# Attention and a gated feed-forward in one kernel: rests of two pairs as one group scaled on VectorE, two chunks of scores ahead of the rests at the first norm, and the output weights' sums on GpSimd

## The chip, the cores and the metric

The kernel runs on one core of a Trainium2 chip, in float32. The metric is the device time of one execution in microseconds; lower is better. The core has five engines with queues of their own: TensorE (matrix products; PE in the profile, PEld for its weight loads), VectorE (DVE), ScalarE (ACT), GpSimd (POOL) and SyncE (SP, which here issues nearly all transfers). Each runs its own instructions in the order in which the program gave them and waits for the others by semaphores. TensorE writes to PSUM, the others work on SBUF and, but for GpSimd, on PSUM.

## The reference

Queries and keys are normalised over the head, attention follows, and its output, put back into rows, goes through a normalised SwiGLU feed-forward.

```python
batch, n_heads, seq, head_dim = (8, 12, 448, 64)
n_tokens, d_model, d_ff = (3584, 768, 1536)

q_n, k_n = (rmsnorm(q, g_q), rmsnorm(k, g_k))
scores = scale * np.matmul(q_n, k_n.transpose(0, 1, 3, 2))
scores = scores - np.max(scores, axis=-1, keepdims=True)
attn = np.exp(scores)
attn = attn / (np.sum(attn, axis=-1, keepdims=True) + 1e-09)
out = np.matmul(attn, v)
...
xn = x / rms * rms_g
g = xn @ w_gate
silu = g * (1.0 / (1.0 + np.exp(-g)))
val = xn @ w_val
return silu * val @ w_out
```

## The kernel before

The work is cut into 48 pairs of heads, six to each of the 8 sequences (`g` counts pairs, `b, hp = divmod(g, 6)`). A pair's 448 positions are three full blocks of 128 and a rest of 64. The rests of all six pairs of a sequence lie in one tile, `rest`, and so they are normalised together, in groups.

The order of the work is written out by hand. A list of steps on TensorE is made with `pe(fn)`; `after(n, fn)` puts the work of another engine n steps later in the program. An engine's queue is therefore in the order of these calls, whatever the data are doing.

For each pair, `squares` (L461) squares q and k on ScalarE (L470), sums on VectorE (L473) and calls `rms_qk` on GpSimd (L489, L490: the reciprocal root) and `norm_q` (L492), which scales the three blocks of q with two GpSimd products (L495). k is not scaled; its factor goes into the exponential. `norm_rests(b, lo, hi)` (L439) does the same for the rests of pairs lo to hi of a sequence: squares L446, sums L448, the root L451 and L452, and the scaling of q and k L453, the last three on GpSimd. `turn(g, i)` (L499) transposes q with its rests (i = 0: L511, L513; the copies are qT, L514 on ScalarE, and the rests' part of kT, L515 on VectorE) or the blocks of k (i = 1, copy L517).

`score(g, chunks)` (L519) multiplies k and q for chunks of 128 keys, two matmuls each (one for each head, L527), into PSUM tiles of `ps_s`, of which there are four, and ScalarE takes the exponential (L531). `rests(g)` (L552) does this for the 64 last keys of pair g (L557, exponential L572, one tile of `ps_s`) and begins the output of pair g-1 (L563; in the first seven pairs also the sums of exponentials, L568). That output is collected in the one tile of `ps_m`. `values(g)` (L574, L579) adds the other keys, `sums(g)` (L582, L592) the sums of exponentials over the keys. VectorE takes their reciprocal (L596 or L600) and scales the output into `x` (L607), which frees the tile of `ps_m`; ScalarE squares x (L610, L612) and GpSimd adds that up (L613). From pair 7 on the exponentials are added on GpSimd before the sums (L537, L544).

When a sequence's six pairs are done, `rms_x` (L622) and `norm_x` (L633) normalise x: four matmuls (L627), the root (L629, L631), four matmuls that spread it over the partitions (L639), and six products on VectorE (L646). This happens for the first time at pair 7. Then the feed-forward's matmuls come, in pieces that `fill` places between the steps of the attention.

During the first sequences the feed-forward's weights, which are given in float64, are converted in pieces of 128x384 (`convert`, L753: ScalarE L719 and L720, VectorE L725 to L727, GpSimd L763) and stored in DRAM (`kept`, `kept_o`). The first sequence's feed-forward multiplies plainly (L1107, L973). All the later ones use Strassen's scheme with seven products (`quad`, L883, products L878; `out_strassen`, L1012, products L1076). It needs weights that are sums of blocks: those of the gate and value weights are made by `derive` (L822, subtraction L835), those of the output weights by `derive_o` (L843, subtraction L855). They are made once, while the second sequence's feed-forward runs, and stored; derive_o makes four for each of six columns, 24 in all, each 128x384, and each store (L751) waits in SyncE's queue for its subtraction. In the same stretch VectorE adds products (L890), does the gate (L900, L901) and adds blocks of the feed-forward's hidden values (L953 to L956, 128x128), for the output's scheme.

The start, before the loop over the pairs, is:

```python
    squares(0, 0)
    warm(9)
    pe(idle)
    norm_rests(0, 0, 1)
    squares(0, 1)
    pe(lambda: turn(0, 1))
    gains()
    squares(1, 0)
    squares(1, 1)
    warm(3)
    pe(lambda: turn(0, 0))
    norm_rests(0, 1, 3)
```

`warm` issues matmuls on the identity (L1223).

Of the kernel before, what the change touches and what calls it, by code (L numbers as in the profile page):

```python
# [12 lines left out]
ALU = mybir.AluOpType  # L13
# [5 lines left out]
B, H, S, D = 8, 12, 448, 64  # L19
# [3 lines left out]
NPAIR = H // 2  # L23
# [312 lines left out]
def safe_scores(  # L336
# [20 lines left out]
    nc = tc.nc  # L357
# [21 lines left out]
    def after(n, fn):  # L379
        due.append((now["t"] + n, fn))  # L380

    def pe(fn):
        now["t"] += 1
        fn()
        for item in [d for d in due if d[0] <= now["t"]]:
            due.remove(item)
            item[1]()


    NG = B * NPAIR  # L390
# [4 lines left out]
    def own(j):  # L395
        return slice(j * D, (j + 1) * D)
# [42 lines left out]
    def norm_rests(b, lo, hi):  # L439

        if b >= B:
            return
        n = hi - lo
        rest = st["rest", b][:, lo:hi]
        sq = tmp.tile([128, n, 2, D], F32, name="sq", tag="sq", bufs=2)
        nc.scalar.activation(sq, rest, ACT.Square)  # L446
        ms = small.tile([128, n, 2], F32, name="msr")
        after(1, lambda: nc.vector.tensor_reduce(out=ms, in_=sq, axis=AX_X, op=ALU.add))  # L448

        def scale():  # L450
            nc.gpsimd.tensor_scalar(ms, ms, D * 1e-6, None, ALU.add)  # L451
            nc.gpsimd.tensor_tensor(ms, ms, mhalf[:, 0:2 * n].rearrange("p (n h) -> p n h", h=2), ALU.pow)  # L452
            nc.gpsimd.tensor_tensor(rest, rest, ms.unsqueeze(3).to_broadcast([128, n, 2, D]), ALU.mult)  # L453

        after(1 if b == 0 else 2, scale)

    def direct(g):
# [3 lines left out]
    def squares(g, i):  # L461

        if g >= NG:
            return
        n = 2 * NK
        if i == 0:
            st["ms", g] = small.tile([128, 2 * n], F32, name="ms")
        ms = st["ms", g]
        sq = tmp.tile([128, n * D], F32, name="sq", tag="sq", bufs=2)
        nc.scalar.activation(sq, st["qk", g][:, i], ACT.Square)  # L470

        def reduce():
            nc.vector.tensor_reduce(out=ms[:, i * n:(i + 1) * n], in_=sq.rearrange("p (n d) -> p n d", d=D), axis=AX_X, op=ALU.add)  # L473

        after(1, reduce)
        if g <= 1:

            after(1, lambda: rms_qk(g, slice(i * n, (i + 1) * n)))
            if i == 0:
                after(1, lambda: norm_q(g))  # L480
        elif i == 1:
            after(2, lambda: rms_qk(g))
            after(2, lambda: norm_q(g))
# [8 lines left out]
    def norm_q(g):  # L492
        qn = st["qn", g] = qn_pool.tile([128, 2 * NK * D], F32, name="qn")
        for h in range(2):
            nc.gpsimd.tensor_tensor(  # L495
                qn.rearrange("p (t h d) -> p h t d", h=2, d=D)[:, 1 - h], st["qk", g][:, 0].rearrange("p (h t d) -> p h t d", h=2, d=D)[:, h],
                st["rs", g][:, h * NK:(h + 1) * NK].unsqueeze(2).to_broadcast([128, NK, D]), ALU.mult)

    def turn(g, i):  # L499


        if g >= NG:
            return
        b, hp = divmod(g, NPAIR)
        if ("qT", g) not in st:
            for part in ("qT", "kT"):
                st[part, g] = qkT_pool.tile([128, S], F32, name=part)
        src = st.pop(("qn", g)) if i == 0 else st["qk", g][:, 1]
        ps = (ps_m if todo else ps_f).tile([128, 512], F32, name="tr", tag="m" if todo else "f")
        for t in range(NK):  # L510
            nc.tensor.transpose(ps[:, t * 128:(t + 1) * 128], src[:, t * 2 * D:(t + 1) * 2 * D], ident)  # L511
        if i == 0:
            nc.tensor.transpose(ps[:, NK * 128:], st["rest", b][:, hp].rearrange("p h d -> p (h d)"), ident)  # L513
            nc.scalar.activation(st["qT", g], ps[:, 0:S], ACT.Copy, scale=gqk[:, 0:1])  # L514
            nc.vector.tensor_copy(st["kT", g][:, LAST], ps[:, S:])  # L515
        else:
            nc.vector.tensor_copy(st["kT", g][:, FULL], ps[:, FULL])  # L517
# [56 lines left out]
    def values(g):  # L574

        vt, av = st["v", g], st["av", g]
        for c in range(NK):
            for j in range(2):
                nc.tensor.matmul(av[own(j), 0:S], lhsT=vt[:, j, c], rhs=st["e", g, c, j], start=False,  # L579
                                 stop=(c == NK - 1), skip_group_check=True)  # L580
# [123 lines left out]
    def data(key):  # L704
        return st[key][0][:, 0:BW]
# [137 lines left out]
    def derive_o(wait=6):  # L843

        if not sums_o:
            return
        c, (to, plus, minus, place) = sums_o[0]
        for name in BLOCKS:
            if asked.get(("wd", 1, name, c), now["t"]) > now["t"] - wait:
                return  # L850
        sums_o.pop(0)
        a, b = data(("wd", 1, plus, c)), data(("wd", 1, minus, c))
        key = ("wd", 1, to, c)
        st[key] = st[("wd", 1, place, c)]
        nc.vector.tensor_tensor(data(key), a, b, ALU.subtract)  # L855

        def store():
            keep(key)
            asked["sums_o"] = asked.get("sums_o", 0) + 1

        after(1, store)
        if to == "T4":
            for name in ("T1", "T2", "T3", "T4"):
                after(6, lambda name=name: used(("wd", 1, name, c)))
# [360 lines left out]
    def some_rests(g):  # L1225
        b, hp = divmod(g, NPAIR)
        if g == 1:
            norm_rests(0, 3, NPAIR)
        elif hp in (3, 4):
            norm_rests(b + 1, 3 * (hp - 3), 3 * (hp - 2))  # L1230

# [1 line left out]
    squares(0, 0)  # L1233
    warm(9)
    pe(idle)
    norm_rests(0, 0, 1)
    squares(0, 1)
    pe(lambda: turn(0, 1))
    gains()
    squares(1, 0)  # L1240
    squares(1, 1)
    warm(3)
    pe(lambda: turn(0, 0))
    norm_rests(0, 1, 3)
    for g in range(NG + 1):
        b, hp = divmod(g, NPAIR)
        if g:
            load_pair(g + 3)
        if hp == 2:
            for i in range(2):  # L1250
                load_rests(b + 1, i, nc.sync)
            load_v_rests(b + 1)
        if g == 0:
            pe(lambda: score(0, (0,)))
            pe(lambda: rests(0))
            pe(lambda: score(0, (1, 2)))
            squares(2, 0)
            squares(2, 1)
            for i in range(2):
                pe(lambda: turn(1, i))  # L1260
            for _ in range(3):
                convert()
            load_pair(3)
            load_v(2)
            convert()
            load_rows()
            continue
        if g <= NPAIR:
            pe(lambda: score(g, (0,)))
            squares(g + 2, 0)  # L1270
            squares(g + 2, 1)
            convert()
            if g > 1:
                pe(lambda: turn(g + 1, 0))
                some_rests(g)
                pe(lambda: turn(g + 1, 1))
            pe(lambda: rests(g))
            pe(lambda: values(g - 1))
            if g == 1:
                pe(lambda: turn(g + 1, 0))  # L1280
                some_rests(g)
                pe(lambda: turn(g + 1, 1))
            load_v(g + 2)
            convert()
            pe(lambda: sums(g - 1))
            pe(lambda: score(g, (1, 2)))
            convert()
            if g == 2:
                bound()
            continue  # L1290

        pe(lambda: (rests(g), score(g, (0,)) if g < NG else None))
        if g == NPAIR + 1:
            pe(lambda: rms_x(0))
        pe(lambda: values(g - 1))
        load_v(g + 2)
        if g == NPAIR + 1:
            pe(lambda: score(g, (1,)))
            pe(lambda: norm_x(0))
            pe(lambda: score(g, (2,)))  # L1300
        pe(lambda: sums(g - 1))
        if g == NPAIR + 1:
            begin(0, 15)
        elif g < NG:
            pe(lambda: score(g, (1, 2)))
        if hp:
            fill()
            squares(g + 2, 0)
            squares(g + 2, 1)
            pe(lambda: turn(g + 1, 0))  # L1310
            some_rests(g)
            fill()
            pe(lambda: turn(g + 1, 1))
            fill()
            continue
        fill(3)
        pe(lambda: turn(g + 1, 0))
        fill(1)
        pe(lambda: rms_x(b - 1))
        squares(g + 2, 0)  # L1320
        squares(g + 2, 1)
        pe(lambda: turn(g + 1, 1))
        fill(len(todo))
        begin(b - 1, 16)
        pe(lambda: norm_x(b - 1))
        fill()
# [41 lines left out]
```

## Time and profile before

| | us |
|---|---|
| median of 6 runs | 1621.26 (1619.69 to 1623.05) |
| the profiled execution | 1617.73, its span 1615.9 |
| VectorE busy in the span | 864.2 |
| GpSimd busy in the span | 649.6 |
| ScalarE busy in the span | 471.8 |
| TensorE's mean granted clock | 0.996 |

A profile is one execution. Its page lists busy time by engine, then the costliest groups of instructions: the line of the kernel, the engine, the operation, what it writes and reads by the program's names, how often, its busy time and mean duration, and the idle time of the engine ahead of it with what ended that. Other views give the waits by engine, the instructions in order of time, and the busy time of each engine in a stretch, with the clock that TensorE was granted there (1.00 is full speed). Times in the views count from the start of the span. The four longest gaps on TensorE but for the start lie at 344, 373 to 378, 420 and 445 us, while the sums of weights are made. These rows show the sums:

```
L835 DVE TENSOR_TENSOR w<-w,w 128x384 f32<-128x384 f32 x31 | 25.6, 858 | 0.0
L855 DVE TENSOR_TENSOR w<-w,w 128x384 f32<-128x384 f32 x17 | 11.2, 661 | 0.1
L855 DVE TENSOR_TENSOR top<-top,w 128x384 f32<-128x384 f32 x3 | 2.6, 862 | 0.0
L855 DVE TENSOR_TENSOR w<-top,w 128x384 f32<-128x384 f32 x2 | 1.1, 546 | 0.0
L855 DVE TENSOR_TENSOR w<-w,top 128x384 f32<-128x384 f32 x1 | 0.8, 770 | 0.0
L855 DVE TENSOR_TENSOR top<-w,top 128x384 f32<-128x384 f32 x1 | 0.5, 544 | 0.0
```

### The profile page before, as it was taken

To read this page: it belongs to the slowest core of one execution; us is meant where nothing else is said; L and a number is where in the kernel's file an instruction comes from. 1 tells how busy PE (TensorE), PEld (TensorE's weight loads), DVE (VectorE), ACT (ScalarE), POOL (GpSimd) and SP (SyncE) were. 2 spreads that over 40 slices of the span, in tenths; PEclk is the share of its full clock that TensorE was granted. 3 is DMA by queue.
4 is the path that set the end of the run, shared out by engine and by line. 5 is a ranking of instruction groups with operands and counts; after the bars stand their busy time and mean duration, and the time that the engine had idled before them with its cause. 6 is when DMAs were issued, how large, how long until landed. Compare 5 with 4: busy or idle time off the path is not lost.

```text
span 1615.9 us, 21550 instructions
## 1 busy us (share of the span) xinstructions
PE 1585.6 (98%) x7328; PEld 1121.9 (69%) x7328; DVE 864.2 (53%) x1490; ACT 471.8 (29%) x944; POOL 649.6 (40%) x672
## 2 busy tenths in 40 slices
PE   7999999999999999999999999999999999999998
PEld 3344445677865888668875688658886588959974
DVE  4989899378852354425563354524565235433531
ACT  6746564223221232223222222222232122101010
POOL 6867877444432344324533443344343322100000
PEclk9999999999999999999999999999999999999999
DMA  7748574567575555565544655476454454557651
GB/s 192 219 137 252 173 234 142 180 206 235 191 237 157 173 157 151 170 206 162 152 137 132 201 156 158 118 224 186 137 161 130 145 177 118 152 188 232 174 152 49
DMA packets 264586, 276.81 MB, mean 171 GB/s; under 512 B 79124, under 2 KB 261396, under 8 KB 264468
## 3 DMA queue, kind: packets, MB, share of 16 engines
q1 hardware_dynamic: 263540, 275.15, 57.0%
q8 instruction: 60, 0.98, 0.3%
q14 instruction: 58, 0.48, 0.1%
q10 hardware_dynamic: 800, 0.20, 0.1%
q0 software_dynamic: 128, 0.00, 0.0%
HBM read 235.93 MB, written 39.32 MB: 170 GB/s over the span
## 4 chain that ended last, share of the span: by engine, by line
PE 80%; DVE 6%; issue 0%; ACT 0%; POOL 0%; DVEq 0%; ACTq 0%
PE ff L878 39%; PE ff L1076 21%; PE av L579 5%; PE sc L527 5%; PE ff L973 3%; PE sc L557 2%; PE den L592 2%; PE tr L511 1%; DVE rd L600 1%; DVE w L835 1%; DVE top L726 1%; DVE top L727 1%; PE ff L1107 0%; DVE w L855 0%; DVE top L725 0%
## 5 line engine op out<-in xcount | busy, mean ns | idle before, releaser
L878 PE MATMUL ff<-x,w 128*128 128x224 f32 x1704 | 348.7, 353 | 3.0 <-ACT p L911 3.0
L878 PEld LDWEIGHTS ff<-x,w 128*128 128x128 f32 x1704 | 319.7, 190 | 14.1 <-issue 5.9
L537 POOL TENSOR_TENSOR es<-e 128x448 f32<-128x448 f32 x82 | 91.2, 1133 | 522.0 <-ACT e L531 522.0
L878 PE MATMUL ff<-xs,w 128*128 128x224 f32 x1320 | 270.9, 353 | 1.0 <-DVE u L890 1.0
L878 PEld LDWEIGHTS ff<-xs,w 128*128 128x128 f32 x1320 | 247.8, 190 | 5.2 <-issue 3.9
L1076 PE MATMUL ff<-w,h 128*128 128x384 f32 x582 | 200.1, 487 | 0.0
L544 POOL TENSOR_TENSOR es<-es,e 64x448 f32<-64x448 f32 (+1 forms) x164 | 194.0, 1193 | 6.3
L600 DVE RECIPROCAL rd<-rd 128x448 f32<-128x448 f32 x41 | 121.0, 2952 | 126.6 <-ACT rd L599 126.6
L531 ACT ACTIVATE e<-sc,rs 128x448 f32<-128x448 f32 x288 | 161.7, 634 | 52.2 <-PE sc L527 50.4
L1076 PEld LDWEIGHTS ff<-w,h 128*128 128x128 f32 x582 | 109.0, 190 | 76.1 <-DMA vt<-in_v_dram 3.3
L527 PE MATMUL sc<-qT,kT 64*128 64x448 f32 x576 | 138.8, 575 | 3.4 <-DVE kT L517 2.1
L1076 PE MATMUL ff<-w,so 128*128 128x384 f32 x350 | 120.4, 488 | 2.0 <-DVE y L1037 2.0
L579 PE MATMUL av<-e,vt 128*64 128x448 f32 x576 | 118.8, 548 | 0.0
L490 POOL TENSOR_TENSOR rs<-ms,mhalf 128x12 f32<-128x12 f32 (+1 forms) x50 | 114.9, 2297 | 4.2
L527 PEld LDWEIGHTS sc<-qT,kT 64*128 64x128 f32 x576 | 54.3, 186 | 85.0 <-issue 69.0
L1107 PE MATMUL ff<-x,w 128*128 128x448 f32 x288 | 111.8, 541 | 0.0
L1076 PEld LDWEIGHTS ff<-w,so 128*128 128x128 f32 x350 | 65.5, 190 | 48.3 <-DVE y L1037 3.9
L890 DVE TENSOR_TENSOR cc<-ff,u 128x448 f32<-128x448 f32 x84 | 52.3, 623 | 87.5 <-PE ff L878 87.3
L763 POOL TENSOR_TENSOR w<-top,raw 128x384 int32<-128x384 int32 x72 | 77.1, 1082 | 39.4 <-DVE top L727 25.6
L579 PEld LDWEIGHTS av<-e,vt 128*64 128x64 f32 x576 | 37.1, 136 | 76.6 <-issue 75.9
L1107 PEld LDWEIGHTS ff<-x,w 128*128 128x128 f32 x288 | 53.3, 190 | 50.8 <-issue 49.0
L613 POOL TENSOR_TENSOR ss<-ss,rd 128x448 f32<-128x448 f32 x40 | 47.4, 1185 | 77.6 <-ACT rd L612 75.9
(122 smaller groups left out, 1915.6 us busy)
## 6 DMA issues: line engine op xcount, KB each, us to landing
w<-kept SPq DMA_DIRECT2D x477, 192.0 KB, 3.0
w<-kept_o SPq DMA_DIRECT2D x290, 192.0 KB, 2.8
kept<-w SPq DMA_DIRECT2D x86, 192.0 KB, 3.9
top<-kept SPq DMA_DIRECT2D x75, 192.0 KB, 2.6
qk<-in_q_dram SPq DMA_DIRECT2D x48, 192.0 KB, 3.2
qk<-in_k_dram SPq DMA_DIRECT2D x96, 96.0 KB, 3.6
vt<-in_v_dram SPq DMA_DIRECT2D x48, 192.0 KB, 2.5
raw<-in_moe_w_gate_dram SPq DMA_DIRECT2D x24, 384.0 KB, 4.5
```

The costliest lines, as they stand in the source:

```text
L490: nc.gpsimd.tensor_tensor(st["rs", g][:, cols], ms, mhalf[:, cols], ALU.pow)
L527: nc.tensor.matmul(ps[:, 0:S], lhsT=kT[r, c * 128:(c + 1) * 128], rhs=qT[r, :], start=True, stop=True)
L531: nc.scalar.activation(e, ps[:, 0:S], ACT.Exp, scale=rs[:, n:n + 1])
L537: nc.gpsimd.tensor_tensor(es, st["e", g, 0, j], st["e", g, 1, j], ALU.add)
L544: nc.gpsimd.tensor_tensor(es[r], es[r], e[r], ALU.add)
L579: nc.tensor.matmul(av[own(j), 0:S], lhsT=vt[:, j, c], rhs=st["e", g, c, j], start=False, stop=(c == NK - 1), skip_group_check=True)
L600: nc.vector.reciprocal(rd, rd)
L763: nc.gpsimd.tensor_tensor(data(key).bitcast(I32), top, lo, ALU.add)
L878: nc.tensor.matmul(bank[:, w * HT:(w + 1) * HT], lhsT=wt[:, c * 128:(c + 1) * 128], rhs=x[:, c, :], start=onto is None and w == c == 0, st ...
L890: nc.vector.tensor_tensor(add[name], ps[:, 0:S], add[other], ALU.add)
L1076: nc.tensor.matmul(ps, lhsT=a, rhs=data(("wo", b, name, c)), start=first and c == 0, stop=c == NFP - 1, skip_group_check=True)
L1107: nc.tensor.matmul(bank[w][:, 0:S], lhsT=data(key)[:, c * 128:(c + 1) * 128], rhs=st["x", 0, half][:, c, :], start=half == c == 0, stop=ha ...
```

## The change

Three things are changed.

At the start, the rests of the first two pairs are one group. The reciprocal root stays on GpSimd (`root`), the scaling goes to VectorE and is placed by the caller, after the squares of k; the other four pairs of the first sequence are two groups of two, one between the two transposes of pair 1 and one at pair 1's place in the loop. `norm_q` of the first two pairs goes to VectorE.

At pair 7, where x is normalised for the first time, the scores of two chunks come ahead of the rests, then the values, then `rms_x`, the third chunk, `norm_x` and the sums.

In `derive_o`, the subtraction is issued on GpSimd, at the same place in the program.

```diff
@@ norm_rests
-        def scale():
+        first = b == lo == 0
+
+        def root():
             nc.gpsimd.tensor_scalar(ms, ms, D * 1e-6, None, ALU.add)
             nc.gpsimd.tensor_tensor(ms, ms, mhalf[:, 0:2 * n].rearrange("p (n h) -> p n h", h=2), ALU.pow)
-            nc.gpsimd.tensor_tensor(rest, rest, ms.unsqueeze(3).to_broadcast([128, n, 2, D]), ALU.mult)
-
+
+        def scale():
+
+            (nc.vector if first else nc.gpsimd).tensor_tensor(rest, rest, ms.unsqueeze(3).to_broadcast([128, n, 2, D]), ALU.mult)
+
+        after(1 if b == 0 else 2, root)
+        if first:
+            return scale
         after(1 if b == 0 else 2, scale)
@@ norm_q
-            nc.gpsimd.tensor_tensor(
+            (nc.vector if g <= 1 else nc.gpsimd).tensor_tensor(
@@ derive_o
-        nc.vector.tensor_tensor(data(key), a, b, ALU.subtract)
+        nc.gpsimd.tensor_tensor(data(key), a, b, ALU.subtract)
@@ some_rests
-            norm_rests(0, 3, NPAIR)
+            norm_rests(0, 4, NPAIR)
@@ the start
-    norm_rests(0, 0, 1)
+    scale = norm_rests(0, 0, 2)
     squares(0, 1)
+    after(1, scale)
...
-    norm_rests(0, 1, 3)
...
-            for i in range(2):
-                pe(lambda: turn(1, i))
+            pe(lambda: turn(1, 0))
+            norm_rests(0, 2, 4)
+            pe(lambda: turn(1, 1))
@@ the loop, pair 7 (NPAIR + 1)
-        pe(lambda: (rests(g), score(g, (0,)) if g < NG else None))
         if g == NPAIR + 1:
+
+            pe(lambda: score(g, (0, 1)))
+            pe(lambda: rests(g))
+            pe(lambda: values(g - 1))
+            load_v(g + 2)
             pe(lambda: rms_x(0))
-        pe(lambda: values(g - 1))
-        load_v(g + 2)
-        if g == NPAIR + 1:
-            pe(lambda: score(g, (1,)))
+            pe(lambda: score(g, (2,)))
             pe(lambda: norm_x(0))
-            pe(lambda: score(g, (2,)))
-        pe(lambda: sums(g - 1))
-        if g == NPAIR + 1:
+            pe(lambda: sums(g - 1))
             begin(0, 15)
-        elif g < NG:
-            pe(lambda: score(g, (1, 2)))
+        else:
+            pe(lambda: (rests(g), score(g, (0,)) if g < NG else None))
+            pe(lambda: values(g - 1))
+            load_v(g + 2)
+            pe(lambda: sums(g - 1))
+            if g < NG:
+                pe(lambda: score(g, (1, 2)))
```

## The prediction

> **What bounds the kernel now.** I read the busy shares first, then who waited for whom on TensorE over the whole span, then each of the stretches where it waited, and last the granted clock there.
>
> ```profile
> PE 1585.6 (98%) x7328; PEld 1121.9 (69%) x7328; DVE 864.2 (53%) x1490; ACT 471.8 (29%) x944; POOL 649.6 (40%) x672
> ```
>
> TensorE is busy for 98% of the span; only 30.3 us are left to win. The waits, longest first (who waited, for whom, us in total, times, longest):
>
> ```profile
> PE tr L513 <- POOL rest L453: 3.1, 2, 1.7
> PE ff L878 <- ACT p L911: 3.0, 1, 3.0
> PE tr L511 <- DVE kT L515: 2.8, 2, 2.0
> PE ff L878 <- DVE u L890: 2.5, 2, 1.5
> ...
> PE av L563 <- issue: 1.2, 1, 1.2
> ```
>
> The first belongs to the start, the L563 one to the first norm (at 90 us), and most of the rest to 340 to 450 us, where L835 and L855 subtract weights. Stretch by stretch (busy us of each engine, then clock):
>
> ```profile
> 10.00:15.00 5.00, 4.46 (x14) 1.54 (x16) 1.56 (x4) 2.60 (x5) 4.57 (x7) 0.66 0.97 269
> 340.00:350.00 10.00, 6.98 (x37) 6.63 (x36) 9.83 (x20) 2.67 (x7) 5.54 (x4) 1.00 0.52 175
> ```
>
> The columns after the length are PE, PEld, DVE, ACT, POOL. Between 340 and 350 us VectorE (9.83 of 10) is the bound and TensorE waits 3.02 us. And at 10 to 15 us the clock is at 0.66, after two short gaps. What VectorE does when GpSimd works beside it stands in the two engines' timelines (start, us, instruction):
>
> ```profile
> 369.48 0.28 DVE L953 TENSOR_TENSOR so<-h,h 128x128 f32<-128x128 f32 x1
> 369.80 1.11 DVE L954 TENSOR_TENSOR so<-so,h 128x128 f32<-128x128 f32 x1
> 370.83 1.22 DVE L955 TENSOR_TENSOR h<-h 128x128 f32<-128x128 f32 x1
> 371.97 1.22 DVE L956 TENSOR_TENSOR so<-h,so 128x128 f32<-128x128 f32 x1
> 373.11 0.55 DVE L835 TENSOR_TENSOR top<-w,top 128x384 f32<-128x384 f32 x1
> ```
> ```profile
> 365.94 2.22 POOL L537 TENSOR_TENSOR es<-e 128x448 f32<-128x448 f32 x2 [10.94 <-ACT e L531]
> 368.11 0.40 POOL L924 COPY h<-h 128x64 f32<-128x64 f32 x2
> 369.54 1.21 POOL L613 TENSOR_TENSOR ss<-ss,rd 128x448 f32<-128x448 f32 x1 [1.03 <-ACT rd L612]
> 370.71 5.34 POOL L544 TENSOR_TENSOR es<-es,e 128x448 f32<-128x448 f32 x4
> ```
>
> A 128x128 operation of two SBUF tensors takes VectorE 0.28 us alone and 1.1 to 1.2 us once GpSimd's adds run: each waits for the add in progress, and then the two engines alternate, one operation each. This decides the change.
>
> **The output weights' sums on GpSimd (L855, 24 operations).** Removed from VectorE: 24 operations, 16.2 us by their groups (17 at 0.661, 3 at 0.862, 2 at 0.546, one of 0.77, one of 0.54). Added to GpSimd: 24 of 128x384. The nearest row is L763, the same size, 1.00 us at least, 1.02 median; so some 24 us. I go through the four stretches in which TensorE waits, playing GpSimd's new order against VectorE's by the rule that the rows show; TensorE's earlier times are kept, a shift moves all.
>
> A, 334 to 347. VectorE loses three L855 here (3.3 us with their waiting), GpSimd gets two sums between its adds (the other two are ready before 332, when it is idle). VectorE's six L835 are now blocked by seven GpSimd operations instead of five. The wait ends when the first L473 is done (346.19) plus 1.08 us of ScalarE behind it. I find L473 0.8 us earlier: -0.8; bounds -3.0 (all of it) and 0.
>
> C, 366 to 381. No L855 stands before the L835 at 373.11 for which TensorE waits 0.76 us; they come after it. But GpSimd gets three sums there: one right behind L537 (368.16 to 369.16), one behind L613, one between the L544. VectorE's eight 128x128 operations, of which five passed freely, are each blocked now. Three operations of 1.0 us, less what lay in VectorE's own idle time, and one more L544 that now comes ahead: the L835 ends at about 377.3 instead of 373.66, +3.6. TensorE then has 3.25 us of work, and the 1.04 us that it waited at 378.00 for L890 go, since L890 is through by 379.8: net +2.6; bounds -0.5 (only the one L855 ahead of L890 counts) and +4.1.
>
> D, 403 to 422. TensorE waits 1.49 us for L890 at 421.17. Three L855 go (1.6 us), and VectorE reaches the 128x128 operations 1 us earlier; but there GpSimd now runs three sums around its two copies, three blocks of about 1 us each against free passage before. L890 comes 1.0 us later: +1.0; bounds -1.4 and +2.2.
>
> E, 433 to 447. As C, with two sums ahead of the L835 at 440.54 (behind L537 and behind L613): L835 ends 3.8 us later, TensorE's 1.98 us wait for L515 goes, 3 L855 with it: net +1.8; bounds -1.5 and +2.8.
>
> Sum -0.8 + 2.6 + 1.0 + 1.8 = +4.6. Elsewhere (350 to 365, 385 to 396) VectorE had 0.7 to 3.8 us of idle time between its pieces, which covers it. The stores behind each sum wait in SyncE's queue; a later sum delays the loads behind it by at most 2 us (set 2), or 4 us where an L835 is late, against loads that are issued 10 us ahead of their use; I take 0, and 1 us if that cover is gone.
>
> C and E leave TensorE idle for 4.4 and 4.1 us. The clock: gaps of 1.35 and 0.72 us were followed by half clock from about 11.0 to 14.7, gaps of 1.72 and 2.13 by the same at 21.4, 3.02 us at 344 by none. Between 0 and 1.8 us (half of 3.6) each; I take 1.0 each, +2.0.
>
> [...]
>
> **Two chunks of scores ahead of the rests at the first norm.** Before, rests' scores (L557) run at 89.53, and L563 waits 1.20 us until 91.70: its one buffer is read by L607 until 91.59. After, four score matmuls go first; they fill the four score buffers by about 91.5, and the rests' scores then need the first of them back, which is ScalarE's exponential. That stands on ScalarE behind L612 (which waits for L607, 91.69), L719 and L720, so it starts at 93.06 (where L572 starts now) and ends at 93.64. TensorE waits 91.5 to 93.7. From there: L557 and L563 overlapped 0.9, L568 0.9, L579 2.4, L627 0.9 (at 97.9), L527 0.95 to 99.7; L639 needs L631, 2.24 us after L627's start, 100.2, so 0.5 us waits; L639 1.1, L592 2.4: L1107 starts at 103.7, where it was 102.97. +0.7; bounds -1.2 (the old wait gone and no new one) and +2.0.
>
> **The start.** Group of two pairs: L446 0.42 for 0.31, L448 0.42 for 0.29, L452 1.04 for 0.72 (each from the old second group, which is of two pairs, against the old first, of one), and the scaling on VectorE, never seen there; between 0.28 (128x128, two inputs) and 0.55 (128x384), 0.42, for 0.40 on GpSimd. So the first transposed rests come at 10.03, not 9.49: +0.54, and score 0 with it. Then pair 1: its rests no longer hold TensorE up (1.72 us at 17.95), but ScalarE has the qT copy (18.32) only 0.25 us after the squares in front of it; that is all this wait was worth. With its exponentials 0.55 later, qT starts at 18.55, and L517, behind the two L473, lets the scores go at 21.0, not 20.75: +0.25; bounds -0.4 and +0.9. norm_q on VectorE covers idle VectorE time (1.60 us before 6.30); kT's copy waits for it 0.8 us and is needed only at 10.5. The other groups of rests (pairs 2 and 3, then 4 and 5) come in smaller pieces than the old one of three; their transposes did not wait before (27.79, 34.32), and GpSimd is freed of about 1.9 us of qn, so nothing. SyncE's queue keeps its order of transfers.
>
> Sum: 4.6 + 2.0 + 0.7 + 0.25 = +7.5. The profiled execution took 1617.73 us (span 1615.9), 3.5 below the median of the six runs; 1625.3 for its like, and 1621.26 + 7.5 = **1628.8** for the median.
>
> **Rivals.** (1) The sums block little, and VectorE's relief decides: A -3.0, C -0.5, D -1.4, E -1.5, with +0.95 from the other parts: -5.4, 1615.8. For it: most L855 ran at 0.55, unblocked, and GpSimd is idle half the time there. Against: its idle time is not where the waits are. It decides if the sums behind L537 are over before VectorE's 128x128 operations start. Chance 0.14. (2) The two even out, C to E at +0.7 together and no half clock: +0.8, 1622.1. For it: the waits of C and E are replaced by others rather than added to. Chance 0.18. (3) The change does not do what it says where it counts, because GpSimd runs the sums long before (their data are loaded early): then the last sums of C and E fall into idle time; this would end as (1). The order of GpSimd's queue speaks against it, where they stand behind L537, which waits 10.94 us for ScalarE.
>
> **How the numbers follow.** Mine 0.68, (1) with (3) 0.14, (2) 0.18. 0.2% (3.2 us) is about what a measurement of this kernel can tell from no change: slower 0.66, within 0.2, faster 0.14. The range reaches down to case (2) less a little, 1620, and up to the upper bounds of C, D and E with the first norm's, 1633.
>
> **What would show it.** In the changed profile (its lines stand some 8 further down: L863 for L855, L843 for L835, L545 for L537): L863 rows of about 1.0 us on GpSimd between L545 and the adds at 368 and 435; VectorE's four 128x128 operations there at 1.1 us each instead of 0.28; TensorE's wait for the L843 "top" near 373 at 4 us and near 441 again, with a clock below 1.00 behind; the wait for L612 and the exponential instead of L563 near 92, of 2.2 us. I am wrong if VectorE's 128x128 operations stay at 0.28, or if the waits between 340 and 450 us sum to under 8.6 us.

## The result, and the profile after

The changed kernel takes 1625.13 us (median of 18 runs, 1622.05 to 1627.34), the kernel before 1621.01 us beside it (38 runs, 1617.81 to 1623.82). The ratio is 1.0026, with an interval of 1.0019 to 1.0032: 0.26% slower, 4.2 us. The profiled execution after took 1624.15 us (span 1622.1), 1 us under its median; that of before lay 3.3 us under its own, and this will matter.

The page's busy times, then who waited for whom on TensorE (us in total, times, longest):

```profile
PE 1588.8 (98%) x7328; PEld 1125.8 (69%) x7328; DVE 866.4 (53%) x1471; ACT 472.7 (29%) x944; POOL 671.6 (41%) x691
```
```profile
PE ff L886 <- DVE top L843: 6.4, 2, 3.8
PE sc L535 <- ACT top L727: 3.7, 1, 3.7
PE tr L521 <- DVE rest L458: 2.3, 1, 2.3
...
PE ff L886 <- ACT p L919: 1.8, 1, 1.8
PE tr L519 <- DVE kT L523: 1.7, 2, 0.9
...
PE sc L565 <- ACT e L539: 1.6, 1, 1.6
PE ff L886 <- DVE u L898: 1.5, 1, 1.5
```

24 sums of about 1 us came to GpSimd, which gave five operations of the start to VectorE (+22.0 us in all). VectorE, rid of 16.2 us and given these five, is busy for 2.2 us more than before. In the run of the sums alone, further down, it is busy for 864.0 us with 24 operations fewer, where it was 864.2: what it was rid of came back as blocked time. The waits for L843 (the first subtraction of a set, into the tile `top`; "the first difference" from here on) went from 1.1 to 6.4 us, the one for L919 (near 344 us) fell from 3.0 to 1.8. Two waits are new: the one for L539, and one of 0.83 us near 116 us for kT (L523); the one of 1.98 us for kT near 446 us is gone.

The stretches (length, then busy us of PE, PEld, DVE, ACT and POOL, then the granted clock):

```profile
10.00:15.00 5.00, 4.21 (x11) 1.21 (x13) 2.01 (x8) 2.10 (x4) 3.30 (x5) 0.66 0.90 274
340.00:350.00 10.00, 8.24 (x46) 7.85 (x45) 9.83 (x16) 3.16 (x7) 8.01 (x7) 1.00 0.59 198
...
376.40:383.20 6.80, 5.74 (x17) 5.20 (x18) 4.73 (x7) 0.01 (x1) 1.91 (x2) 0.50 0.60 184
...
448.10:451.50 3.40, 3.11 (x8) 2.83 (x9) 3.40 (x5) 0.00 (x0) 2.49 (x2) 0.50 0.32 116
```

From 340 to 350 us VectorE is still full (9.83), but TensorE works 1.26 us more. At 376.4 and 448.1 us the clock is at half, behind the two waits for L843; before it was full there. Why L843 is late stands in the timelines of VectorE and of GpSimd (start, us, instruction):

```profile
369.15 0.81 DVE L961 TENSOR_TENSOR so<-h,h 128x128 f32<-128x128 f32 x1
370.06 0.31 DVE L962 TENSOR_TENSOR so<-so,h 128x128 f32<-128x128 f32 x1
370.30 1.22 DVE L963 TENSOR_TENSOR h<-h 128x128 f32<-128x128 f32 x1
371.44 1.08 DVE L964 TENSOR_TENSOR so<-h,so 128x128 f32<-128x128 f32 x1
372.44 1.22 DVE L961 TENSOR_TENSOR so<-h,h 128x128 f32<-128x128 f32 x1
...
375.92 1.48 DVE L843 TENSOR_TENSOR top<-w,top 128x384 f32<-128x384 f32 x1
```
```profile
368.80 1.01 POOL L863 TENSOR_TENSOR w<-w,w 128x384 f32<-128x384 f32 x1
369.74 0.49 POOL L932 COPY h<-h 128x64 f32<-128x64 f32 x2
370.21 1.15 POOL L621 TENSOR_TENSOR ss<-ss,rd 128x448 f32<-128x448 f32 x1
371.33 1.04 POOL L863 TENSOR_TENSOR w<-w,w 128x384 f32<-128x384 f32 x1
372.33 2.32 POOL L552 TENSOR_TENSOR es<-es,e 128x448 f32<-128x448 f32 x2
```

The sums stand between GpSimd's other work, and the two engines alternate: VectorE's 128x128 operation that starts at 371.44 ends 0.15 us behind the sum begun at 371.33, the next one about when the first of GpSimd's adds does. That is the picture the prediction drew. At pair 7, ScalarE's timeline and TensorE's:

```profile
91.81 0.58 ACT L620 ACTIVATE rd<-x 128x448 f32<-128x448 f32 x1 [0.63 <-DVE x L615]
92.29 0.53 ACT L727 ACTIVATE top<-raw 128x384 f32<-128x384 f32 x1
92.73 0.53 ACT L728 ACTIVATE raw<-raw 128x384 int32<-128x384 uint32 x1
93.16 2.19 ACT L539 ACTIVATE e<-sc,rs 128x448 f32<-128x448 f32 x4
```
```profile
87.91 4.33 PE L535 MATMUL sc<-qT,kT 64*128 64x448 f32 x16
93.83 0.59 PE L565 MATMUL sc<-qT,kT 64*64 64x448 f32 x2 [1.59 <-ACT e L539]
```

The scores of pair 6's last two chunks and of the two that go ahead are one row of TensorE's. Then the rests' scores wait for the first exponential, which stands behind L620, L727 and L728, until 93.83 us.

Where the two profiled executions part can be read from one instruction that each pair has, the transposition of its rests (L513, after the change L521), after minus before in us:

```
pair   2 to 7   8      9 to 16       17     18, 19  20 to 47
       +0.2     +0.81  +1.86..+1.94  +6.05  +4.99   +6.36
```

By this, the start costs 0.2, pair 7 costs 0.6 and 1.05 more, and the stretch of the sums 4.4. **This reading is misleading**, as the experiments show.

### The profile page after: what moved, and what is told of

It reads as the page before. It is cut to its first block, busy times and chain, and to the rows that moved or that the text cites. A ratio compares the mean times of both kernels' runs of the same rounds, so it can differ in the third digit from the quotient of the medians.

```text
span 1622.1 us, 21564 instructions
## 1 busy us (share of the span) xinstructions
PE 1588.8 (98%) x7328; PEld 1125.8 (69%) x7328; DVE 866.4 (53%) x1471; ACT 472.7 (29%) x944; POOL 671.6 (41%) x691
## 4 chain that ended last, share of the span: by engine, by line
PE 80%; DVE 5%; DMA 1%; issue 0%; POOL 0%; ACT 0%; SPq 0%; DVEq 0%; POOLq 0%; ACTq 0%
PE ff L886 39%; PE ff L1084 21%; PE sc L535 5%; PE av L587 5%; PE ff L981 3%; PE sc L565 2%; PE den L600 2%; PE tr L519 1%; DVE top L734 1%; DVE rd L608 1%; DVE top L735 1%; DVE w L843 1%; PE ff L1115 0%; DVE top L733 0%; PE rb L647 0%
## 5 line engine op out<-in xcount | busy, mean ns | idle before, releaser
L545 POOL TENSOR_TENSOR es<-e 128x448 f32<-128x448 f32 x82 | 91.3, 1135 | 493.0 <-ACT e L539 493.0
L539 ACT ACTIVATE e<-sc,rs 128x448 f32<-128x448 f32 x288 | 161.8, 635 | 53.0 <-PE sc L535 46.9
L771 POOL TENSOR_TENSOR w<-top,raw 128x384 int32<-128x384 int32 x72 | 77.4, 1087 | 38.9 <-DVE top L735 25.5
L886 PE MATMUL ff<-x,top 128*128 128x224 f32 x312 | 70.5, 363 | 7.9 <-DVE top L843 6.4
```

The costliest lines, as they stand in the source:

```text
L539: nc.scalar.activation(e, ps[:, 0:S], ACT.Exp, scale=rs[:, n:n + 1])
L545: nc.gpsimd.tensor_tensor(es, st["e", g, 0, j], st["e", g, 1, j], ALU.add)
L771: nc.gpsimd.tensor_tensor(data(key).bitcast(I32), top, lo, ALU.add)
L886: nc.tensor.matmul(bank[:, w * HT:(w + 1) * HT], lhsT=wt[:, c * 128:(c + 1) * 128], rhs=x[:, c, :], start=onto is None and w == c == 0, st ...
```

## The experiments

### Each part alone

The diff's three parts, each put into the kernel before by itself.

```diff
start_only:  norm_rests (root, scale), norm_q on VectorE, some_rests, the start
norm_only:   the branch for g == NPAIR + 1 in the loop
sums_only:
-        nc.vector.tensor_tensor(data(key), a, b, ALU.subtract)
+        nc.gpsimd.tensor_tensor(data(key), a, b, ALU.subtract)
```

> The kernel before with the change's start alone. By the two traces the start put TensorE 0.23 us later at the first score of pair 1 and left that offset unchanged to pair 7. Theory (the parts add): 1621.0 + 0.2 = 1621.2 us. Rival (the half clock after the start's longer gap of 3.71 us is worth more in most executions): 1622 us or more.

> The kernel before with the change's order at pair 7 alone. Theory (the parts add): the offset of the two traces grew by 0.6 us up to pair 8's transposes and by 1.05 us behind them, where TensorE waits 0.83 us for a copy of kT that stands behind a conversion: 1621.0 + 1.65 = 1622.7 us, with that second wait in its trace. Rival (the second wait comes from another phase of the conversions that the start brought, not from pair 7): 1621.6 us, and no wait near 115 us.

> The kernel before with the 24 subtractions on GpSimd alone. Theory (the parts add, the sums are the rest of 4.1): 1621.0 + 2.2 = 1623.2 us; waits near 373 and 445 us of 3.8 and 2.6 us for the first-part difference, half clock behind both. Rival (the sums carry all of it, and pair 7's loss is absorbed): 1625 us. Second rival (the sums cost nothing by themselves and gain 1.3 us near 344): 1620 us.

Measured, against 1621.29 us (33 runs of the kernel before; the last column is the ratio's share of that):

| part alone | median, us | ratio and interval | in us |
|---|---|---|---|
| start | 1621.66 | 1.0006, 0.9998 to 1.0015 | +1.0 (-0.3 to +2.4) |
| order at pair 7 | 1625.41 | 1.0030, 1.0020 to 1.0039 | +4.9 (+3.2 to +6.3) |
| sums on GpSimd | 1621.62 | 1.0004, 0.9995 to 1.0014 | +0.6 (-0.8 to +2.3) |

The order at pair 7 carries the loss, not the sums, though sums_only shows the very waits of the changed kernel (6.4 us for the first difference, 1.8 for L911). Neither theory had this: the first was 2.7 us too low for pair 7, its +2.2 us for the sums lies at the edge of their interval, and "the sums carry all" is refuted. The three parts add to 6.5 us by the ratios and to 4.8 by the medians, the whole change has 4.2; within these intervals the parts add. What the profiled executions hide is visible in the clock behind the wait near 344 us, which is 3.02 us long in both of these; first the kernel before, then start_only, which does the same work there (columns as above):

```profile
346.00:349.40 3.40, 2.13 (x11) 2.13 (x12) 3.37 (x8) 0.94 (x2) 2.50 (x2) 1.00 0.51 160
```
```profile
347.20:350.60 3.40, 2.90 (x8) 2.65 (x9) 3.26 (x9) 0.44 (x2) 3.20 (x3) 0.50 0.47 162
```

The same wait is followed by full clock in one execution and by 3.41 us of half clock in the other, and TensorE falls 1.41 us behind. The clock changes at steps 3.41 us apart (in the profile of before half clock begins at 11.15, 21.39 and 79.42 us, 3 and 17 steps apart), and where these steps lie differs from execution to execution. In the profile of before a step at 345.66 us (78 steps behind the one at 79.42 us, where that execution has half clock) cuts the gap (344.25 to 347.27) into 1.41 and 1.61 us; in start_only 2.52 us of it lie in one step. Of the eight profiled executions in this study with a wait of 3.0 to 3.1 us there, six had half clock behind it; of the six with 1.70 to 1.76 us (VectorE relieved there), none. Likewise the wait of 1.97 us near 446 us: half clock in six of seven, and the kernel before's profile was the seventh. So the profile of before was a lucky execution, 3.3 us under its median, and every difference to it held that luck as well. In one place it had bad luck: a gap of 1.38 us on TensorE, at 77.4 us, had half clock behind it (from 79.42 us), as in only two others of the 14 profiled executions.

### The clock: idle matmuls in the long waits

```diff
         x = st["left", b][left]
+        if b == 1 and right == "T3" and fp in WARM:    # WARM = {2: 9, 5: 6}
+            for _ in range(WARM[fp]):
+                nc.tensor.matmul(bank[:, 0:HT], lhsT=ident, rhs=x[:, 0, :], start=True, stop=True, ...)
```

> The changed kernel with idle matmuls (9 ahead of one product near 373 us, 6 ahead of one near 445 us, 0.38 us each) in the two long waits of TensorE, into the bank that the product then starts anew; results as before. Theory (the half clock behind the waits is what costs, 2.9 and 1.6 us in the profiled execution; the waits themselves replace others): 1625.1 - 3.5 = 1621.6 us, the clock 1.00 from 340 to 455 us, and a smaller spread from run to run. Rival (the waits cost, the clock follows whatever is done): 1625 to 1626 us.

1621.71 us; ratio to the kernel before 1.0006 (0.9996 to 1.0016), where the changed kernel has 1.0026: 0.20%, 3.2 us better. TensorE's timeline and the stretch:

```profile
375.30 3.57 PE L886 MATMUL ff<-x,ident 128*128 128x224 f32 x18
379.55 1.40 PE L890 MATMUL ff<-x,top 128*128 128x224 f32 x6 [0.68 <-DVE top L844]
```
```profile
370.00:384.00 14.00, 13.32 (x71) 12.57 (x71) 13.62 (x20) 2.82 (x6) 10.33 (x11) 1.00 0.34 110
```

The first difference is as late as ever: the product starts at 379.55 us where it started at 377.46, and this execution was 1.84 us behind already at pair 16. Only the gap is filled, and the clock stays at 1.00. So the half clock behind the waits is what costs, not the waits alone. The two profiled executions say the same: from pair 16 to pair 20 the changed kernel's loses 4.4 us on that of before, this one 1.3, and the 3.1 us between them are the half clock's. The spread from run to run did not become smaller (1619.16 to 1624.08). In this execution half clock is left at the start and, for 3.41 us, behind the wait at pair 7 (from 94.50 us).

### The sums, in two halves

```diff
sums_part:
+        (nc.gpsimd if c in (0, 1, 3) else nc.vector).tensor_tensor(data(key), a, b, ALU.subtract)
sums_rest:
+        (nc.gpsimd if c in (2, 4, 5) else nc.vector).tensor_tensor(data(key), a, b, ALU.subtract)
```

> The kernel before with the sums of three of the six columns on GpSimd (columns 0, 1 and 3, which run near 318 to 339, 352 to 358 and 392 to 397 us), the other three on VectorE. Theory: the wait near 344 us falls from 3.02 to 1.75 us, too short for half clock behind it, and the waits near 374 and 446 us stay at 0.75, 1.04 and 1.98 us: 1621.2 - 1.3 - 1.3 = 1618.6 us. Rival (the columns are not independent; the later stores shift the first-part differences near 373 us): 1621 us, with a wait near 373 us above 2 us.

> The kernel before with the sums of the other three columns (2, 4 and 5) on GpSimd, columns 0, 1 and 3 on VectorE. Theory (moving all 24 cost about nothing because two effects cancel: three columns gain, three lose): the wait near 344 us stays at 3.0 us, the waits near 373 and 445 us become some 3.8 and 2.6 us with half clock behind the first always and behind the second often; slower than the kernel before by 2 to 4 us, about 1624.5 us. Rival (the gain at 344 us has to do with all six, or nothing is lost near 373 and 445 us): within 1 us of the kernel before.

sums_part: 1617.79 us, ratio 0.9976 (0.9967 to 0.9986). sums_rest: 1624.97 us, ratio 1.0025 (1.0015 to 1.0035). As the first theory had it, both times. Their waits, sums_part first:

```profile
PE ff L878 <- ACT p L911: 1.8, 1, 1.8
...
PE ff L878 <- DVE top L835: 1.1, 2, 0.8
```
```profile
PE ff L878 <- DVE top L835: 6.4, 2, 3.8
PE ff L878 <- ACT p L911: 3.0, 1, 3.0
```

Columns 0, 1 and 3 shorten the wait near 344 us and leave the others alone. Columns 2, 4 and 5 leave that one and make the two long waits for L835; in the profiled execution, which lay 3.7 us above its median, the wait near 429 us grew as well, from 1.49 to 2.08 us, with half clock behind it. The gain of one half (3.9 us) and the loss of the other (4.1 us) cancel, and this is why all 24 together cost almost nothing.

### Is it the reading of SBUF?

The kernel before, with one more GpSimd operation of about 1 us beside each sum, which itself stays on VectorE:

```diff
add_beside:
+        nc.gpsimd.tensor_tensor(junk (128x384), ident..., ident..., ALU.add)
pow_beside:
+        nc.gpsimd.tensor_tensor(junk[:, 0:4], ones[:, 0:4], mhalf[:, 0:4], ALU.pow)
```

> The kernel before, the sums still on VectorE, with one more GpSimd addition of 128x384 beside each of the 24, on constants, its result unused. Theory (a GpSimd operation that reads two SBUF tensors holds up VectorE's operations on two SBUF tensors for its whole length): VectorE's eight 128x128 operations near 370 us take 1.1 to 1.2 us each, not 0.28 as half of them before, TensorE's wait for the first-part difference there grows from 0.75 us to 3 to 6 us, and the time by 4 to 10 us. Rival (what counts is GpSimd's own lateness): its additions come later, VectorE's operations keep their 0.28 and 0.55 us.

> As the run with the additions, but each of the 24 is a power of 128x4 on GpSimd, of about the same length (1.0 us) with few elements read. Theory (it is the reading of SBUF, not GpSimd's being busy): VectorE's operations near 370 us last as before, the waits near 373 us stay under 1.5 us, the time within 1.5 us of the kernel before. Rival (GpSimd's own lateness counts): the waits and the time as in the run with the additions.

add_beside: 1630.02 us, ratio 1.0047 (1.0032 to 1.0063). pow_beside: 1621.25 us, ratio 0.9999 (0.9990 to 1.0008). VectorE's timeline near 370 us and one row of GpSimd's beside it, with the additions and with the powers:

```profile
376.26 1.11 DVE L957 TENSOR_TENSOR so<-so,h 128x128 f32<-128x128 f32 x1
377.29 1.21 DVE L958 TENSOR_TENSOR h<-h 128x128 f32<-128x128 f32 x1
378.43 0.91 DVE L959 TENSOR_TENSOR so<-h,so 128x128 f32<-128x128 f32 x1
...
378.32 0.87 POOL L857 TENSOR_TENSOR junk<-ident 128x384 f32<-128x384 f32 x1
```
```profile
368.59 1.10 DVE L956 TENSOR_TENSOR so<-so,h 128x128 f32<-128x128 f32 x1
369.62 0.28 DVE L957 TENSOR_TENSOR h<-h 128x128 f32<-128x128 f32 x1
369.82 0.28 DVE L958 TENSOR_TENSOR so<-h,so 128x128 f32<-128x128 f32 x1
...
369.50 1.06 POOL L857 TENSOR_TENSOR junk<-ones,mhalf 128x4 f32<-128x4 f32 x1
```

With the additions five of the eight operations took 0.91 to 1.22 us, one 0.61 and two 0.3, where all eight were expected to be slow (before it were three). TensorE's wait there grew to 2.37 us, less than the 3 to 6 expected, but one near 427 us to 4.02; the time grew by 7.6 us, as expected. With the powers, seven took 0.28 to 0.32 us; a power runs on GpSimd from 369.50 to 370.56 us, and the two rows of 0.28 us shown ran beside it at their full speed. The one of 1.10 us stood beside an addition (L613). So here an addition on GpSimd holds VectorE up (0.91 to 1.22 us where 0.28 are enough) and a power of the same length does not. Whether that is the addition's reading is not shown: the power reads 4 elements of a partition where the addition reads 384, but it is also another operation. GpSimd's own lateness is not the cause: the powers delay its adds at least as much (1.0 to 1.3 us each, the additions 0.83 to 0.87).

### Pair 7: which wait, and a milder order

```diff
norm_bank (with the new order):
-            ps = ps_s.tile([128, 512], F32, name="sc", tag="s")
+            own_bank = g == NPAIR + 1
+            ps = (ps_f if own_bank else ps_s).tile([128, 512], F32, name="sc", tag="f" if own_bank else "s")
norm_one (with the old order):
-        pe(lambda: (rests(g), score(g, (0,)) if g < NG else None))
+        if g == NPAIR + 1:
+            pe(lambda: score(g, (0,)))
+            pe(lambda: rests(g))
+        else:
+            pe(lambda: (rests(g), score(g, (0,)) if g < NG else None))
```

> Pair 7's new order alone, but the rests' scores of pair 7 go into one of the three banks that the feed-forward uses instead of one of the four score banks, so they need not wait for an exponential. Theory (the wait near 92 us for a score bank, 2.27 us and half clock behind it in the run with the full wait, is most of the loss of this part): the wait falls under 0.3 us and the time to 1622.2 us or less. Rival (the loss comes later, from the second wait near 117 us and what the shift does to the stretch from 340 to 450 us): 1624.5 us or more, though the wait near 92 us is gone.

> The kernel before with one chunk of scores, not two, ahead of the rests at pair 7, all else as before. The four score banks then still have one free for the rests' scores. Theory: TensorE's wait of 1.2 to 1.9 us for the bank of the output falls to 0.3 to 0.9 us, as 0.95 us of scores go ahead of it: 1621.2 - 0.9 = 1620.3 us. Rival (any score chunk that goes first makes the rests' exponential later and a wait moves behind): 1621.5 us or more.

Against 1622.14 us beside them, norm_bank took 1619.95 us (ratio 0.9991, 0.9982 to 1.0000) and norm_one 1619.21 us (0.9985, 0.9976 to 0.9994). TensorE at pair 7, in norm_only and then in norm_bank:

```profile
87.37 4.33 PE L527 MATMUL sc<-qT,kT 64*128 64x448 f32 x16
93.97 0.70 PE L557 MATMUL sc<-qT,kT 64*64 64x448 f32 x2 [2.27 <-ACT e L531]
```
```profile
86.56 4.33 PE L527 MATMUL sc<-qT,kT 64*128 64x448 f32 x16
90.82 0.59 PE L558 MATMUL sc<-qT,kT 64*64 64x448 f32 x2
```

With a bank of its own, the wait is gone, and a part that lost 0.30% is, if anything, a gain of 0.09%. In norm_only's profile half clock stood behind the wait (94.33 us, for 3.41 us), and up to pair 8 the two executions differ by 3.8 us: 2.27 of wait, and the half clock. The second wait, 0.83 us, is in norm_only, in norm_bank and in the changed kernel, but in none with the old order; so it comes from the new order. VectorE's timeline in norm_only shows it:

```profile
116.82 1.38 DVE L727 SCALAR_TENSOR_TENSOR top<-raw,top 128x384 int32<-128x384 int32 x1
118.12 0.21 DVE L515 COPY kT<-tr 128x64 f32<-128x64 f32 x1
```

The copy stands behind a conversion, which takes 1.38 us beside GpSimd's adds instead of 0.56. One chunk ahead instead of two leaves a score bank free: the wait there falls to 0.41 us, from 1.88 in six other executions of the old order, and the gain of 2.4 us (1.0 to 3.9) is above the 0.9 expected. The profiled execution shows only 0.4 us of it: from pair 7 to pair 8 it makes up 1.02 us on that of before, those six 0.60. A new wait of 0.48 us for the sum of squares (L613) takes part of the rest back, and where most of the 2.4 us comes from stays open. In the profile of before that wait was 1.20 us, 0.68 less, because TensorE had lost time to half clock at 79.42 us; the changed kernel's had the same, and 1.59 us where norm_only waits 2.27.

### Versions that beat both

```diff
part_one:     sums_part and norm_one together
part_one_kt:  part_one, and in turn():
-            nc.vector.tensor_copy(st["kT", g][:, LAST], ps[:, S:])
+            if g > NPAIR + 1:
+                nc.scalar.copy(st["kT", g][:, LAST], ps[:, S:])
+            else:
+                nc.vector.tensor_copy(st["kT", g][:, LAST], ps[:, S:])
```

> Both of the two: one chunk ahead at pair 7 and three columns' sums on GpSimd. Theory (the two add): 1617.7 us. Rival (one of them does nothing): 1618.6 to 1620.3 us.

> One chunk ahead at pair 7, columns 0, 1 and 3 on GpSimd, and from pair 8 on the copy of the rests' part of kT on ScalarE instead of VectorE, where it stands behind other work while TensorE waits for its bank. Theory: the waits of 0.83 us near 243 us and 1.97 us near 442 us go, and the half clock that often follows the second: 1616.9 - 2.8 - 0.8 = 1613.3 us. Rival (TensorE then waits for VectorE a little later for the same work): 1616 to 1617 us.

part_one: 1616.88 us, ratio 0.9973 (0.9962 to 0.9985), 0.9 us under sums_part's median beside it, but by the intervals not told from it. By the ratio it gains 4.4 us where its two parts gained 3.9 and 2.4; the intervals leave open whether they add. part_one_kt: **1613.70 us** (1613.39 to 1614.76), ratio 0.9952 (0.9939 to 0.9966). The waits of 0.84 us near 244 and 1.97 us near 442 us are gone, and with the second its half clock; a new wait of 0.85 us at 206 us takes part of that back.

## Why the prediction was right, and where it was not

The direction and the range held: 1625.13 us where 1628.8 was forecast and 1620 to 1633 stated. But the sum was made of the wrong terms, and that it came out is luck: by the runs of the parts, the sums were forecast 6.0 us too dear (+6.6 for +0.6) and the first norm 4.2 us too cheap (+0.7 for +4.9), and the two errors nearly cancel.

- **The start, +0.25.** The traces show +0.23 at pair 1's first score, and the part alone cannot be told from that (-0.3 to +2.4).
- **First norm, +0.7.** The step as stated was right: the wait for the exponential behind L612, L719 and L720, and the 0.4 us for L639; up to pair 8 the traces differ by +0.6. That agreement is luck too: both executions had half clock at 79.4 us, and TensorE, late by it, waited 1.59 us where norm_only's waits 2.27 with half clock behind. The term was mis-sized by two omissions. A wait of 2.2 us was given no half clock, although gaps of 1.72 and 2.13 us at the start had been priced with one. And the kT copy behind the conversions (1.05 us at pair 9) was not looked for, because the replay stopped at L1107. Alone, this part costs +4.9 us (3.2 to 6.3). Up to pair 9 norm_only's execution loses 2.8 us on that of before, half clock included, and 3.4 on the six other executions of the old order, which had no half clock at 79 us; that lies inside the interval.
- **The sums, +4.6 by stretch.** Idle time changed by -1.26 in A (forecast -0.8), +2.0 in C (+2.6), 0 in D (+1.0) and +0.3 in E (+1.8): together +1.05, and +1.3 in after_warm, at full clock throughout. So the stretches were priced more than 3 us too high; this step failed, in D and E above all. In C five of the eight 128x128 operations were blocked (three before), not each. D came out even: two sums from 423.49 us blocked two 128x128 operations (2.1 us for 0.6), and three L855 (1.7 us) were gone. E was wrong because the first sum ran early, at 436.24, and the wait that went (1.98) nearly paid for the one that came (2.58).
- **Half clock, +2.0.** In the profiled execution TensorE worked 5.8 of 6.83 us at half clock behind C and 3.1 of 3.41 behind E: 2.9 + 1.6 = 4.5 us of work, of which 3.1 us reached TensorE's later work (4.4 less 1.3, as above). This is the other step that failed: the price of half clock was taken from one execution, with "3.02 us at 344 by none" as evidence that a long gap may be free, and the half clock that the kernel before itself pays there was put at nothing. That the gap was free was the accident of that execution. In six of eight executions the gap at 344 us did cost, and in six of seven the one at 446. sums_only's execution falls 3.3 us behind that of before over this stretch; of these, 6/8 x 1.41 + 6/7 x 1.68 = 2.5 us are what before's was spared. Some 0.6 is to be added for half clock that sums_only's was spared at 447 us: it stood behind this wait in two of three executions and cost them 0.8 and 1.0 us. By this estimate the sums cost +1.4, inside the measured +0.6 (-0.8 to +2.3), and far from +6.6.
- **The signs.** L863 rows of 1.0 us behind L545, blocked 128x128 operations (five of eight at 1.07 to 1.22 us near 370, one at 0.81), waits of 3.83 us at 373 and 2.58 at 446 with half clock behind: all there, but that the wait near 92 us was 1.6 and not 2.2 us. The waits from 340 to 450 us sum to 9.7 us, above the 8.6 that would have refuted the step. A profile can show each stated sign and still not show what decides the time.
- **Rivals.** Rival (2), "the two even out", is what the sums did by themselves, though not as it was argued: half clock is in it on both sides. Rival (1) is true of columns 0, 1 and 3 alone. Rival (3) holds for single sums: those at 365.66 and 436.24 us ran ahead of L545, the others in C and E behind it.

## What to carry to other kernels

Before a wait is priced from one profile, ask whether that execution lies at its median; here it lay 3.3 us below, mostly because gaps of 2 and 3 us had, by chance, no half clock behind them. In these executions a TensorE gap that had 2.08 us or more inside one step of the clock cost itself and 0.8 to 1.7 us more for each step of half clock behind it. So cutting one from 3 to 1.7 us is worth some 2.4 us by these figures (an estimate: 1.3 and six eighths of 1.41), cutting one from 1.3 to nothing 1.3. And a move of work to GpSimd is to be decided place by place, by whether it blocks the VectorE operations that TensorE waits for next: one half of these sums gained 0.24%, the other, which runs beside the operations ahead of the first differences, lost 0.25%.

## What the runs showed of the hardware

In the profiles the clock's steps are 3.41 us long and not tied to the program: the first half-clock step lay at 11.15, 12.69, 19.23 or 9.54 us in different executions. Taking the gaps of TensorE after the start in all 14 profiled executions, each of the 15 that had 2.08 us or more inside one step was followed by half clock, of 3.41 or 6.83 us (in the changed kernel's profile 2.79 us of one gap lie in the step ahead of 376.42 us, where half clock begins for 6.83 us, and 2.29 us of another in the step ahead of 448.10, for 3.41 us). Below 2 us it went both ways (1.99 us without, 1.35 us with).

The timed runs carry it too: among the 33 runs of the kernel before, a mean clock of 0.996 goes with 1618.1 to 1619.0 us, and 0.991 to 0.993 with 1622.0 to 1624.2 us. So most of what looks like noise of 6 us goes with the mean clock, as more or fewer steps of half clock would make it; the timed runs have no traces that show the steps.
